# Small vector work of a two-dimensional Fourier mix moved from VectorE to GpSimd, with a new order of all operations

## The chip, the core and the metric

The kernel runs on one core of a Trainium2 chip. A core has five engines with a queue each, and every queue is worked through in order: TensorE (PE, with its weight loads shown apart as PEld), VectorE (DVE), ScalarE (ACT), GpSimd (POOL) and SyncE (SP). SP here only issues transfers. Matmuls write to PSUM, eight banks of 128 x 512 floats; DVE and ACT copy results from there to SBUF, and POOL is given only operands in SBUF.

The metric is device time in microseconds of one execution. Three runs of the kernel before gave 113.83, 114.42 and 114.73 us, median 114.42.

## The reference

```
def _A_ref(x, w_r, w_i):                      # _B_ref is the same
    X = rfft2(x.astype(float32), axes=(-2, -1))
    X = X * (w_r + 1j * w_i)
    return irfft2(X, s=(S, D), axes=(-2, -1)).astype(bfloat16)

x = A_x                                       # 1 x 2048 x 1024, bfloat16
g = sigmoid((x * gate_w).sum(-1, keepdims=True))
return g * _A_ref(x, A_w_r, A_w_i) + (1 - g) * _B_ref(x, B_w_r, B_w_i)
```

Both branches transform the same input; `B_x` is not used. So one forward transform serves both, its result is multiplied by two sets of complex weights, and the inverse transform of both is mixed by a gate per row.

## The kernel before, in words

The 2048 rows are split as 128 x 16 and the 1024 columns by symmetry into quarters, so that every transform becomes a chain of matmuls with constant matrices. Even and odd columns of the spectrum are apart from the first step on (`e` and `o`; later `par` 0 and 1).

*Folds.* For each of 16 slices `s1` and each half, `F1:s:par:bank` (L336) multiplies the input with a cosine and sine matrix. The result in PSUM has two parts whose sum and difference are wanted (`fold`, L422, two operations of 256 columns). For most, ACT or DVE copies one part to a scratch tile `wx` (`FC`, L201 on ACT, L203 on DVE) and DVE folds the other from PSUM with it (`FD`); for eight of them both parts are copied (`FX`) and POOL folds (`FP`).

*Products.* Sixteen units `n` follow, eight even and eight odd. Per unit: `F2` (L528) twice, evictions `T`; `F3` (L569), eviction `X`; on DVE the product `P:n` (`prod`, L586, 128 x 4096), which multiplies `X` with the weights of both branches. Column 0 of the product is special: a small matmul `Y` (L599, L601) and a small DVE product `NA` (`patch_mul`, L609) make its two terms in a buffer `np` of which there are two in turn, and the patch sum `N` (`patch`, L615, 16 columns) adds them into the product tile. Then `J:n` (L632) runs the first step of the inverse transform from the patched product. Its result is evicted in two halves `R`, and stored to a scratch tensor in DRAM (`H`, L654). The product tile has three buffers.

`F3` needs a negated copy `wn` of a constant; `neg:engine:from:to` (L280) makes it in two parts, 256 and 768 columns.

*The gate.* `gc` (L285 to L297) prepares coefficients from `gate_w` on POOL; `GH`, `GC`, `Gt`, `GK`, `GZ` bring the row sums to all partitions, `GS` (L485, ACT) takes the sigmoid into `EA`. Then, for four groups of four slices, `GA:engine:first` (L515) multiplies `EA` with a constant matrix and `GB` (L519) subtracts it from that matrix into `EB`, 128 x 512 each: eight operations.

*The end.* `L:par:v` (L665) loads the scratch back with rows and columns exchanged, once every `H` of that half has landed. `V` (L675) applies `EA` and `EB`, which mixes the branches; eviction `VC`; the last step is `C` or `U` (L712, L703). Even results are evicted to `EV` (`E`, `ES`, `EF`, or `EX` with sums `EQ`, L806). Odd results are added to and subtracted from them: `OR` (L826) on DVE straight from PSUM; `QD` (L833, DVE) with `QP` (L838, DVE or POOL); or `OC` with `OP` (L822, POOL). `S:v` (L847) stores two slices.

What sets the order is one string, `ORDER`, of such tokens. The program is recorded token by token, each engine's queue keeps that order, and semaphores follow the data. A token carries the engine (`A`, `D`, `P`, or `S` for a transfer) and the PSUM bank where there is a choice. The operations that the change moves:

```
Q[e].tensor_scalar(t, s, -1.0, None, ALU.mult)                         # neg
Q[e].tensor_tensor(Ps[n]...[:, :, 0], t[:, :, 0], t[:, :, 1], ALU.add) # N
Q[e].tensor_tensor(C["EA"][:, s], C["EA"][:, s], E4, ALU.mult)         # GA
Q[e].tensor_tensor(C["EB"][:, s], E4, C["EA"][:, s], ALU.subtract)     # GB
```

Here `E4` is the constant `E` repeated four times. All operands lie in SBUF.

Of the kernel before, what the change touches and what calls it, by code (L numbers as in the profile page):

```python
# [29 lines left out]
FC:11:e:A FD:9:o W:S:1 c:S:WJ:0:4 c:S:EZ FC:10:e:A F1:13:e:5 FD:9:e FD:11:e c:S:WJ:4:16 FX:7:o:A F1:12:e:1 FP:5:o FD:10:e  # L30
F1:8:o:4 F1:15:e:7 FC:13:e:A FC:12:e:A FD:13:e F1:14:e:3 F1:14:o:2 F1:6:o:5 W:S:0 W:S:7 FC:8:o:A FC:15:e:A FP:7:o F1:12:o:6
FD:12:e F1:13:o:0 FD:15:e F1:15:o:1 W:S:2 FC:14:e:A FX:6:o:A FC:14:o:A FD:14:e FD:8:o neg:D:0:4 F2:1:0:3 FC:12:o:A FC:13:o:A
F1:10:o:7 F2:0:1:5 FC:15:o:A T:1:0:A F2:1:1:4 FC:10:o:A FD:13:o FD:12:o F2:0:0:0 F1:11:o:3 T:0:1:A neg:D:4:16 FD:15:o T:1:1:A
T:0:0:A c:S:FD:1:2 F3:1:4 F3:0:0 F2:2:0:6 FC:11:o:A pw:P FD:10:o FD:14:o X:1:A F2:4:0:7 FD:11:o F2:3:0:2 W:S:3 P:1:b W:S:10
FP:6:o X:0:A F2:2:1:5 T:2:0:A F2:3:1:4 F2:4:1:3 T:2:1:A T:3:0:A Y:0:1 Y:1:0 F3:2:5 NA:1:D P:0:b GH:2 T:3:1:A X:2:A T:4:1:A
F3:3:3 N:1:D NA:0:D T:4:0:A J:1:6:0 GC:A Gt:5 X:3:A P:2:b GK:D N:0:D R:1:1:A Y:2:4 Y:3:2 R:1:0:A F2:7:0:3 NA:2:D NA:3:D
F2:5:0:5 F2:5:1:1 T:5:0:A P:3:b T:5:1:A F3:4:6 F2:7:1:2 X:4:A T:7:0:A J:0:0:4 T:7:1:D N:3:D R:0:1:A N:2:D R:0:0:D J:3:2:6
R:3:0:A R:3:1:D P:4:b GZ:0:0 F3:5:4 GS:0 X:5:A Y:4:7 NA:4:D F2:6:1:6 J:2:0:2 T:6:1:A R:2:1:A GZ:1:4 R:2:0:D Y:5:6 N:4:D GS:1
# [5 lines left out]
T:12:0:A F3:11:6 T:12:1:A J:8:4:2 P:10:b T:14:1:A X:11:A F2:13:0:1 F2:14:0:0 F3:12:6 T:14:0:D R:8:0:A R:8:1:A X:12:A H:5:0
H:5:1 H:7:1 H:7:0 H:6:0 H:6:1 T:13:0:D W:S:12 F2:13:1:0 L:0:0 L:0:7 L:0:1 J:9:2:4 T:13:1:A L:0:4 L:0:2 R:9:0:A P:11:b
J:10:0:6 L:0:5 R:10:0:A R:9:1:D F2:15:1:3 V:0:0:1:2 F3:14:0 R:10:1:A X:14:A T:15:1:A J:11:4:6 V:0:0:0:0 F2:15:0:3 L:0:6 H:8:1
R:11:1:A H:8:0 R:11:0:A P:12:b VC:0:0:1:D T:15:0:A C:0:0:1:2 VC:0:0:0:D P:14:b F3:13:6 E:0:1:D J:12:0:4 V:0:2:1:3 X:13:A
R:12:1:A H:9:0 V:0:1:1:7 C:0:0:0:6 V:0:2:0:4 VC:0:1:1:A C:0:1:1:7 VC:0:2:1:A F3:15:2 VC:0:2:0:A R:12:0:D P:13:b EX:1:1:A
J:14:0:4 H:10:1 H:9:1 X:15:A R:14:1:A H:10:0 H:11:0 H:12:1 E:0:0:D J:13:6:2 P:15:b R:14:0:A V:0:1:0:5 R:13:0:A H:12:0 H:11:1
R:13:1:D C:0:2:1:4 J:15:0:6 VC:0:1:0:A EX:2:1:A R:15:0:A GB:D:8 R:15:1:D C:0:1:0:5 EX:1:0:A V:0:6:0:4 C:0:2:0:3 EQ:2:1:0:D  # L50
V:0:6:1:1 VC:0:6:0:A V:0:5:1:0 H:14:1 V:0:5:0:5 EX:2:0:D H:14:0 H:13:1 H:13:0 C:0:6:0:7 VC:0:6:1:A VC:0:5:1:A H:15:0 E:6:0:A
H:15:1 VC:0:5:0:A C:0:6:1:4 C:0:5:1:1 E:6:1:A L:0:3 EQ:2:0:0:D ES:5:1:D L:1:3 EQ:1:1:1:P EQ:1:1:0:P V:0:4:1:6 V:0:4:0:2
V:0:7:1:5 C:0:5:0:3 EQ:2:1:1:P EQ:1:0:1:P VC:0:4:1:A EF:5:1 VC:0:4:0:D ES:5:0:D L:1:1 L:1:0 C:0:4:1:0 EQ:2:0:1:P EF:5:0
C:0:4:0:7 V:0:7:0:6 VC:0:7:1:A C:0:7:1:4 V:0:3:1:5 VC:0:7:0:D V:0:3:0:1 C:0:7:0:3 ES:4:1:A ES:4:0:A EF:4:0 EX:7:1:D
VC:0:3:1:A C:0:3:1:7 VC:0:3:0:A EX:7:0:A V:1:3:1:5 V:1:3:0:2 C:0:3:0:3 E:3:1:D L:1:5 L:1:6 L:1:7 L:1:2 VC:1:3:1:A VC:1:3:0:A
EQ:1:0:0:P EQ:7:1:0:P C:1:3:1:7 EQ:7:0:1:P C:1:3:0:2 EF:4:1 E:3:0:A EQ:7:0:0:P QD:3:1:1 V:1:1:1:0 L:1:4 QD:3:0:1 VC:1:1:1:A
V:1:1:0:1 V:1:0:0:6 U:1:1:1:0 VC:1:1:0:A VC:1:0:0:A V:1:0:1:3 C:1:0:0:6 QD:3:1:0 QD:3:0:0 U:1:1:0:5 VC:1:0:1:A V:1:6:1:2
OC:1:0:A EQ:7:1:1:P QP:3:1:1:D C:1:0:1:3 VC:1:6:1:A OR:1:1:1 OR:1:1:0 V:1:5:0:1 V:1:6:0:5 V:1:5:1:2 QD:0:0:1 QD:0:0:0
# [853 lines left out]
```

## Time and profile before

| | |
|---|---|
| median of three runs | 114.42 us |
| the profiled execution | 113.75 us, span 111.9 us |
| PE busy | 97.9 us (87%) |
| DVE busy | 99.3 us (89%) |
| ACT busy | 86.0 us (77%) |
| POOL busy | 40.7 us (36%) |
| DVE product L586, 16 times | 36.4 us, 2.28 us each |
| DVE patch sum L615, 8 times | 1.5 us, 0.22 us each |
| DVE gate operations L515 and L519, 8 times | 3.3 us, 0.42 us each |
| DVE negation L280, twice | 0.83 and 0.34 us |

The span is the part of an execution from its first to its last instruction in the profile; 1.85 us of the execution's time lie around it. An operation's duration is longer than what it takes of its engine, because the next one starts before the former has ended; the distance between two starts is what it costs the engine. Busy shares are means over stages with different limits, so the stages have to be read apart. In a row of the timeline the columns are start, duration, engine, line, operation, output and inputs by the program's names with partitions x elements and type, and the count; a bracket gives idle time before and what ended it. In a row of the groups the busy time of the group, the mean duration in nanoseconds and the idle time before follow the count.

### The profile page before, as it was taken

How to read it: one execution, taken by the hardware profiler on the slowest of the kernel's cores; microseconds unless marked ns; L12 is line 12 of the kernel's file. 1: busy time of each engine (PE TensorE's matmuls, PEld its weight loads, DVE VectorE, ACT ScalarE, POOL GpSimd, SP SyncE). 2: the span in 40 equal slices, each digit the busy share in tenths (PEclk: the TensorE clock that was granted, in tenths of full speed). 3: DMA queues.
4: the chain of work that ended last, by engine and by line, in shares of the span. 5: the costliest groups of instructions: out<-in, count | busy, mean ns of one | idle time of the engine just before them, and what ended most of it. 6: DMA issues, size and time to landing. Idle time of an engine off the chain costs nothing.

```text
span 111.9 us, 3817 instructions
## 1 busy us (share of the span) xinstructions
PE 97.9 (87%) x1559; PEld 69.9 (62%) x1559; DVE 99.3 (89%) x159; ACT 86.0 (77%) x141; POOL 40.7 (36%) x63
## 2 busy tenths in 40 slices
...
DVE  0079899999999999999999999999959799999970
ACT  4174597999999999999999999999975965554400
POOL 1079999500000000000000000054740689999970
...
DMA packets 17794, 36.79 MB, mean 329 GB/s; under 512 B 1904, under 2 KB 10736, under 8 KB 17776
## 3 DMA queue, kind: packets, MB, share of 16 engines
...
q8 instruction: 12, 0.20, 0.7%
...
q14 instruction: 6, 0.05, 0.1%
...
## 4 chain that ended last, share of the span: by engine, by line
DVE 31%; PE 30%; DMA 16%; issue 8%; POOL 6%; ACT 4%; SPq 1%; DVEq 1%; ACTq 0%; POOLq 0%
DVE p L586 13%; PE ps L675 10%; DMA sc<-rl 9%; DVE y L422 9%; PE ps L712 7%; DMA re<-sc 6%; PE ps L703 5%; POOL y L422 5%; PE ps L245 3%; DVE ot L826 3%; ACT rl L201 2%; PE ps L632 2%; DVE rl L203 1%; SPq L665 1%; ACT X L201 1%
## 5 line engine op out<-in xcount | busy, mean ns | idle before, releaser
L806 POOL TENSOR_TENSOR re<-wx 128x256 f32<-128x256 f32 x10 | 8.8, 900 | 60.6 <-ACT wx L201 53.5
L201 ACT CAST rl<-ps 128x1024 bf16<-128x1024 f32 x24 | 23.9, 1043 | 1.2 <-PE ps L632 0.7
L201 ACT CAST V<-ps 128x512 bf16<-128x512 f32 x28 | 15.6, 602 | 7.6 <-PE ps L675 4.9
L201 ACT COPY wx<-ps 128x256 f32<-128x256 f32 (+1 forms) x38 | 15.3, 458 | 7.9 <-PE ps L336 4.2
L632 PE MATMUL ps<-p,wj 32*64 32x512 bf16 x512 | 17.7, 380 | 2.9 <-DVE re L203 1.0
L528 PE MATMUL ps<-fd,y 128*128 128x256 bf16 x128 | 17.3, 273 | 1.7 <-DVE T L203 0.6
L586 DVE TENSOR_TENSOR p<-X,ro 128x4096 bf16<-128x4096 bf16 x8 | 18.2, 2280 | 0.0
L422 DVE TENSOR_TENSOR y<-ps,wx 128x256 bf16<-128x256 f32 x48 | 16.6, 415 | 1.5 <-ACT wx L201 1.5
L201 ACT CAST X<-ps 128x1024 bf16<-128x1024 f32 x16 | 16.8, 1057 | 0.5 <-DVE p L586 0.2
L336 PE MATMUL ps<-f,re 128*128 128x128 bf16 x256 | 15.3, 220 | 1.1 <-ACT wx L201 1.1
L336 PEld LDWEIGHTS <-re 128*128 128x128 bf16 x256 | 14.8, 99 | 2.0 <-issue 1.7
L201 ACT CAST T<-ps 128x512 bf16<-128x512 f32 x27 | 15.6, 623 | 0.3 <-PE ps L528 0.2
L528 PEld LDWEIGHTS <-y 128*128 128x128 bf16 x128 | 11.4, 97 | 6.5 <-issue 4.7
L632 PEld LDWEIGHTS <-wj 32*64 32x64 bf16 x512 | 8.4, 103 | 9.1 <-issue 5.9
L422 POOL TENSOR_TENSOR y<-wx 128x256 bf16<-128x256 f32 x16 | 11.1, 731 | 5.4 <-DVE wx L203 5.4
L838 POOL TENSOR_TENSOR ot<-pq 128x512 bf16<-128x512 f32 x9 | 12.0, 1361 | 0.5 <-DVE pq L833 0.5
L712 PE MATMUL ps<-ig,V 128*128 128x256 bf16 x88 | 12.2, 273 | 0.0
L569 PE MATMUL ps<-T,wf 64*64 64x512 bf16 (+1 forms) x128 | 10.0, 333 | 1.5 <-ACT rl L201 0.9
L826 DVE TENSOR_TENSOR ot<-re,ps 128x512 bf16<-128x512 f32 x16 | 9.9, 675 | 0.0
L703 PE MATMUL ps<-ig,V 128*128 128x512 bf16 x40 | 9.9, 379 | 0.0
L203 DVE CAST rl<-ps 128x1024 bf16<-128x1024 f32 x8 | 9.7, 1218 | 0.1
L586 DVE TENSOR_TENSOR p<-X,wx 128x4096 bf16<-128x4096 bf16 x4 | 9.1, 2283 | 0.0
...
## 6 DMA issues: line engine op xcount, KB each, us to landing
...
```

The source lines that it names most:

```text
L201: nc.scalar.copy(out=out, in_=in_)
L203: Q[e].tensor_copy(out=out, in_=in_)
L336: nc.tensor.matmul(o, lhsT=lh, rhs=rh, start=(h == 0), stop=(h == 1))
L422: Q[e].tensor_tensor(yo[:, v, k:k + n, s1, :], a.rearrange("p (k c) -> p k c", c=4), b.rearrange("p (k c) -> p k c", c=4), op)
L528: nc.tensor.matmul(ps[:, v * 256:v * 256 + 256], lhsT=y[:, v, par, b, 2 * t:2 * t + 2, :, :].rearrange("p j s c -> p (j s c)"), rhs=C["FD" ...
L586: nc.vector.tensor_tensor(p[:], xb, wb, ALU.mult)
L632: nc.tensor.matmul(o, lhsT=lh, rhs=src[r, ri, wi, tt], start=(q == 0), stop=(q == 3))
L675: nc.tensor.matmul(ps[:, ch * 128:ch * 128 + 128], lhsT=RR[par][:, v, ch // 2, s, c0 + 256 * ab:c0 + 256 * ab + 128], rhs=Ew[:, s1, :], st ...
L703: nc.tensor.matmul(ps, lhsT=Vs[par, v][:, s, ch, :], rhs=rh, start=(ch == 0), stop=(ch == 3))
L712: nc.tensor.matmul(ps[:, o:o + 256], lhsT=Vs[par, v][:, s, ch, :], rhs=g[:, o:o + 256], start=(ch % 2 == 0), stop=(ch % 2 == 1))
L826: nc.vector.tensor_tensor(otile(v)[:, s, h, :], EV[:, v, s], PS["O", 1, v, s], (ALU.add, ALU.subtract)[h])
L838: Q[e].tensor_tensor(otile(v)[:, :, h, 256 * g:256 * g + 256], t[:, :, 0], t[:, :, 1], (ALU.add, ALU.subtract)[g])
```

## The change

Only `ORDER` differs; all functions stay. The counts by engine:

| | before | after |
|---|---|---|
| `neg` | 2 DVE | 2 POOL |
| `N`, patch sums | 8 DVE | 1 DVE, 7 POOL |
| `GA` | 4 DVE | 2 DVE, 2 POOL |
| `GB` | 4 DVE | 1 DVE, 3 POOL |
| `FC` | 1 DVE, 23 ACT | 3 DVE, 21 ACT |
| `T` | 5 DVE, 27 ACT | 8 DVE, 24 ACT |
| `R` | 8 DVE, 24 ACT | 7 DVE, 25 ACT |
| `E` | 3 DVE, 3 ACT | 1 DVE, 5 ACT |
| `EX` | 2 DVE, 4 ACT | 1 DVE, 5 ACT |
| `EQ` | 2 DVE, 10 POOL | 4 DVE, 8 POOL |
| `QP` | 3 DVE, 9 POOL | 2 DVE, 10 POOL |

All other operations keep their number and engine (`VC` is 4 on DVE and 28 on ACT in both, but before `P:15` two were on DVE and now one is). Banks are dealt anew. The gate's coefficients `gc` come ahead of POOL's first fold and ahead of the small memset of `tab`, which ACT's first activation reads. Most weight loads `W` come earlier in SP's queue. In DVE's queue the stretch from `P:1` to `P:15` was

```
P:1 NA:1 P:0 N:1 NA:0 P:2 GK N:0 NA:2 NA:3 P:3 T:7:1 N:3 N:2 R:0:0 R:3:1 P:4 NA:4 R:2:0 N:4 NA:5 P:5
GA:12 GA:0 N:5 P:7 T:9:1 GA:4 NA:7 P:6 NA:6 N:7 N:6 T:10:1 P:8 GB:12 R:6:0 GA:8 GB:4 P:9 GB:0 P:10
T:14:0 T:13:0 P:11 R:9:1 P:12 VC:0:0:1 VC:0:0:0 P:14 E:0:1 R:12:0 P:13 E:0:0 P:15
```

and is now

```
P:1 NA:1 P:0 NA:0 P:2 NA:2 NA:3 GK P:3 T:7:1 R:0:0 R:3:1 P:4 NA:4 R:2:0 P:5 NA:5 N:5
P:7 NA:7 P:6 NA:6 GA:0 GA:12 T:9:1 T:10:1 GB:0 P:8 R:6:0 P:9 T:12:0 P:10
T:13:0 T:13:1 P:11 R:9:1 P:12 T:15:1 VC:0:0:0 T:15:0 P:14 R:12:0 P:13 P:15
```

while POOL, which had nothing between `FP:6` and the first `EQ`, now has

```
N:1 N:0 N:3 N:2 N:4 N:7 GB:12 N:6 GA:8 GB:8 GA:4 GB:4
```

The last 14 operations of POOL are ten `QP` and four `OP`; before there were nine and four. The core of the diff:

```
-warm:8 c:A:F1 x:S:0:1 x:S:1:1 F1:0:o:0 F1:0:e:5 F1:1:e:3 F1:1:o:1 c:A:gws FX:0:o:D x:S:2:2 tab:A x:S:4:2 F1:2:e:2 x:S:6:2
...
-NA:7:D P:6:b H:4:0 H:4:1 NA:6:D F3:9:4 N:7:D N:6:D T:10:1:D J:7:6:0 P:8:b X:9:A R:7:1:A J:6:2:4 R:7:0:A GB:D:12 R:6:0:D
-F3:10:0 R:6:1:A F2:11:0:7 GA:D:8 X:10:A T:11:0:A F2:12:0:2 F2:11:1:5 F2:12:1:0 F2:14:1:1 GB:D:4 P:9:b GB:D:0 T:11:1:A
...
+warm:8 c:A:F1 x:S:0:1 x:S:1:1 c:A:gws gc:P F1:0:e:7 F1:0:o:5 x:S:2:2 tab:A x:S:4:2 F1:1:o:6 x:S:6:2 FC:0:e:D FD:0:e x:S:8:2
...
+neg:P:0:4 F1:10:e:3 FX:7:o:A FP:4:o F1:10:o:4 FP:7:o F1:14:e:5 FC:13:e:A FC:10:e:A F1:12:e:7 F1:15:e:0 FD:13:e F1:6:o:6
+F1:13:o:1 FC:14:e:A neg:P:4:16 FC:15:e:A pw:P FD:10:e FC:10:o:A FD:14:e FC:12:e:A FD:15:e F1:12:o:2 FD:12:e FD:10:o F1:14:o:3
...
+GA:D:12 T:9:1:D T:10:1:D F3:9:4 GB:D:0 H:4:0 X:9:A H:2:0 P:8:b J:7:6:0 R:7:0:A GB:P:12 N:6:P GA:P:8 J:6:2:4 GB:P:8 R:7:1:A
+F2:11:0:7 GA:P:4 R:6:1:A F2:11:1:6 R:6:0:D H:5:1 F2:12:1:0 H:4:1 H:5:0 H:7:0 H:7:1 T:11:1:A F3:10:2 T:11:0:A P:9:b F2:12:0:4
...
+P:14:b J:12:0:4 VC:0:1:1:A X:13:A V:0:2:1:3 C:0:0:0:6 C:0:1:1:7 R:12:1:A V:0:2:0:5 VC:0:2:1:A F3:15:2 EX:1:1:A VC:0:2:0:A
...
+OR:7:1:1 OR:4:1:1 OR:4:1:0 S:S:6 S:S:7:1 S:S:4
```

More of the change, by code (lines that the diff above doesn't have):

```diff
@@ L30 @@
[L30 to L38, printed above, removed]
@@ L44 @@
[L44 to L53, printed above, removed]
@@ L54 @@
[L54 to L58, printed above, removed]
@@ L64 @@
-OP:4:0:0 OR:7:1:0 S:S:7:1 OR:4:1:0 OR:4:1:1 S:S:4
+warm:8 c:A:F1 x:S:0:1 x:S:1:1 c:A:gws gc:P F1:0:e:7 F1:0:o:5 x:S:2:2 tab:A x:S:4:2 F1:1:o:6 x:S:6:2 FC:0:e:D FD:0:e x:S:8:2
+F1:1:e:3 FX:0:o:D FC:1:e:D c:S:WF:0:4 c:S:E FX:1:o:A x:S:10:2 F1:3:e:6 x:S:12:2 x:S:14:2 F1:2:o:5 c:S:WF:4:16 FC:3:e:A FD:1:e
+F1:2:e:2 FD:3:e F1:3:o:4 F1:5:e:7 F1:4:e:1 c:S:FD:0:1 FX:2:o:A F1:5:o:3 F1:7:e:5 c:S:w0 c:S:WJ:0:4 FP:1:o F1:6:e:6 c:S:EZ
+c:S:PM W:S:0 FC:2:e:A FP:0:o FD:2:e W:S:1 c:S:FD:1:2 W:S:7 W:S:3 W:S:2 W:S:5 W:S:4 c:S:WJ:4:16 FC:5:e:A FD:5:e FC:4:e:A
@@ new lines @@
+F1:9:o:2 F1:8:o:0 FC:7:e:A FD:4:e FC:6:e:A FX:5:o:A F1:8:e:7 FC:9:o:A FP:2:o FP:5:o FD:7:e FD:6:e FC:8:o:A FX:3:o:A F1:9:e:3
+F1:4:o:1 F1:7:o:5 FC:9:e:A FD:9:o FC:8:e:A FD:8:o FD:9:e FD:8:e F1:11:e:2 FX:4:o:A FC:11:e:A FD:11:e F1:13:e:6 FP:3:o
+neg:P:0:4 F1:10:e:3 FX:7:o:A FP:4:o F1:10:o:4 FP:7:o F1:14:e:5 FC:13:e:A FC:10:e:A F1:12:e:7 F1:15:e:0 FD:13:e F1:6:o:6
+F1:13:o:1 FC:14:e:A neg:P:4:16 FC:15:e:A pw:P FD:10:e FC:10:o:A FD:14:e FC:12:e:A FD:15:e F1:12:o:2 FD:12:e FD:10:o F1:14:o:3
+FX:6:o:A FC:12:o:A FD:12:o F1:15:o:0 F2:1:0:7 FC:15:o:D FC:14:o:A FC:13:o:A FD:14:o FD:13:o F2:0:0:5 F2:1:1:4 F2:0:1:6
@@ new lines @@
+F1:11:o:2 T:1:0:A T:0:0:A T:1:1:A T:0:1:A FC:11:o:A F3:1:4 F3:0:6 X:1:A FD:15:o X:0:A FD:11:o P:1:b F2:2:0:1 F2:3:1:3 Y:1:0
+F2:2:1:5 F2:3:0:2 T:2:0:A NA:1:D Y:0:7 FP:6:o T:2:1:A T:3:1:A F2:4:1:6 F2:4:0:1 N:1:P F3:2:4 T:3:0:A T:4:0:A GH:3 X:2:A
+F3:3:4 T:4:1:A P:0:b NA:0:D GC:A J:1:6:0 F2:7:0:3 X:3:A P:2:b N:0:P R:1:1:A Y:2:4 Gt:5 Y:3:2 R:1:0:A NA:2:D F2:5:0:4 T:5:0:A
+F2:5:1:0 NA:3:D F3:4:6 GK:D P:3:b F2:7:1:2 T:7:1:D N:3:P N:2:P T:5:1:A J:0:0:4 X:4:A T:7:0:A J:3:2:6 R:0:1:A R:0:0:D W:S:6
+R:3:1:D W:S:10 W:S:8 P:4:b GZ:0:0 F3:5:4 R:3:0:A GS:0 W:S:9 c:S:IG W:S:11 Y:4:7 F2:6:1:6 X:5:A T:6:1:A J:2:0:2 F2:6:0:6
@@ new lines @@
+T:12:1:A F3:11:6 T:12:0:D F2:14:0:0 X:10:A X:11:A F2:14:1:1 J:8:4:2 T:14:1:A H:6:0 H:6:1 T:14:0:A W:S:13 L:0:0 F3:12:6
+F2:13:0:1 L:0:1 L:0:6 L:0:2 R:8:0:A R:8:1:A P:10:b GB:P:4 F2:13:1:0 J:9:2:4 X:12:A R:9:0:A T:13:0:D T:13:1:D L:0:5 J:10:0:6
+R:10:0:A L:0:7 L:0:4 F2:15:1:3 V:0:0:1:2 P:11:b H:8:0 H:8:1 R:9:1:D F3:14:0 R:10:1:A X:14:A J:11:4:6 VC:0:0:1:A P:12:b H:9:0
+H:9:1 V:0:0:0:1 H:10:0 H:10:1 R:11:1:A F2:15:0:2 T:15:1:D C:0:0:1:0 VC:0:0:0:D R:11:0:A V:0:1:1:3 E:0:1:A F3:13:6 T:15:0:D
+P:14:b J:12:0:4 VC:0:1:1:A X:13:A V:0:2:1:3 C:0:0:0:6 C:0:1:1:7 R:12:1:A V:0:2:0:5 VC:0:2:1:A F3:15:2 EX:1:1:A VC:0:2:0:A
```

30 lines of the change are left out of this document (18 added, 12 removed).

## The prediction

> **What bounds the kernel now.** I read the page's forty slices first, one digit for the busy tenths of 2.8 us:
>
> ```profile
> DVE  0079899999999999999999999999959799999970
> ACT  4174597999999999999999999999975965554400
> POOL 1079999500000000000000000054740689999970
> ...
> DVE p L586 13%; PE ps L675 10%; DMA sc<-rl 9%; DVE y L422 9%; PE ps L712 7%; DMA re<-sc 6%; PE ps L703 5%; POOL y L422 5%; PE ps L245 3%; DVE ot L826 3%; ACT rl L201 2%; PE ps L632 2%; DVE rl L203 1%; SPq L665 1%; ACT X L201 1%
> ```
>
> There are three stages. To 25 us DVE folds, beside POOL. From 25 to 77 us DVE has next to no idle time and ACT some 1.6 us, while POOL stands still: these two engines are the bound, and the product (L586) is the longest item of the chain that ended last, whose shares are the last line. From 77 us PE is full until its matmuls end near 104; behind it DVE and POOL finish the output together. That last point decides much here, so I took the ends from the timeline of each engine:
>
> ```profile
> 99.24 6.19 POOL L838 TENSOR_TENSOR ot<-pq 128x512 bf16<-128x512 f32 x5
> 105.60 2.73 POOL L822 TENSOR_TENSOR ot<-re,wx 128x512 bf16<-128x512 f32 x2 [0.17 <-ACT wx L201]
> ...
> 105.90 2.47 DVE L826 TENSOR_TENSOR ot<-re,ps 128x512 bf16<-128x512 f32 x4
> ```
>
> POOL ends at 108.33, DVE at 108.37; the last store takes the rest to 111.9. Since 90.91 POOL has run 13 operations with hardly a gap.
>
> Next the question that the change raises: can POOL work beside DVE? Before, POOL does nothing during the products but at their end, so I put both timelines side by side there, and where DVE made the negated constants beside POOL's folds:
>
> ```profile
> 72.13 2.28 DVE L586 TENSOR_TENSOR p<-X,y 128x4096 bf16<-128x4096 bf16 x1
> 74.33 0.68 DVE L203 COPY re<-ps 128x512 f32<-128x512 f32 x1
> 74.93 2.28 DVE L586 TENSOR_TENSOR p<-X,y 128x4096 bf16<-128x4096 bf16 x1
> ...
> 73.43 1.57 POOL L806 TENSOR_TENSOR re<-wx 128x256 f32<-128x256 f32 x1 [52.39 <-ACT wx L201]
> 76.77 1.03 POOL L806 TENSOR_TENSOR re<-wx 128x256 f32<-128x256 f32 x1 [1.78 <-DMA sc<-rl]
> ...
> 19.61 1.42 POOL L422 TENSOR_TENSOR y<-wx 128x256 bf16<-128x256 f32 x2
> ...
> 20.29 0.83 DVE L280 TENSOR_SCALAR wn<-wf 128x256 bf16<-128x256 bf16 x1
> ...
> 22.36 0.34 DVE L280 TENSOR_SCALAR wn<-wf 128x768 bf16<-128x768 bf16 x1
> ```
>
> POOL's L806 takes 0.72 us at its shortest. The one issued at 73.43, inside a product, ends at 75.00: the product's 74.33 plus 0.67. The next, issued inside the product that gives way at 77.13, ends at 77.80, again 0.67 later. DVE waits likewise: 256 columns of L280 took 0.83 us beside a fold that ended at 21.03, 768 columns 0.34 with POOL idle. So a POOL operation that reads SBUF and a DVE operation with both inputs in SBUF exclude each other, whole instruction by whole instruction. DVE's evictions from PSUM show no such wait.
>
> The Trainium skill (SBUF — State Buffer, Who interferes with whom) says the same: GpSimd and a DVE instruction with two SBUF inputs share a port that is locked for the whole instruction, and whichever issues first keeps it. The trace agrees in these three places; that order of issue decides speaks for the forecast below against its first rival.
>
> **The change, part by part.** Sums are made on the profiled execution (113.75 us, span 111.9). DVE durations are pitches, start to start: product 2.20 (25.28 to 27.48), T or V eviction 0.60, R eviction 1.13, gate operation 0.35, patch sum 0.09.
>
> *Folds.* The two negations leave DVE: 0.75 and 0.27, -1.0. Two more FC copies come to it at 0.38, +0.8. On POOL the negations are covered by their use: the first F3 needed them at 23.06, and the nearest rows (L320, 0.35 for 32 columns; L422, 0.73 for 256) put them at 0.35 to 2.1 us each on an engine idle from 21.03. The gate's coefficients now stand ahead of POOL's first fold and ahead of the memset that ACT's first activation waits for. Their input lands at 1.14 + 3.6 = 4.7 us; POOL's first arithmetic was seen at 6.20, so that chain of 1.1 us ends between 5.8 and about 8.5, against ACT's first copy at 6.32. Cover is ACT's idle time in this stage (3.5 us) and the copies that DVE now makes for itself first; without it, up to 1 us. I take -0.2, bounds -0.7 and +1.0.
>
> *Products, work of DVE up to the last one.* Seven patch sums, 7 x 0.09 = -0.6. Of the gate's operations, seven stood before the last product and three do now: -1.4. Evictions dealt anew: T from 5 to 8 (+1.8), V from 2 to 1 (-0.6), E from 2 to 0 (-1.25), R 6 as before: -0.05. Together -2.05. ACT's share of the same stretch falls by 3 T (1.5) and an FC (0.4) and grows by a V and an E (1.0): -0.9. X:15 ended 0.66 before the product that uses it began, so -1.5 is the most that ACT allows.
>
> *What the moved work costs in its new place.* The rows for POOL:
>
> ```profile
> L838 POOL TENSOR_TENSOR ot<-pq 128x512 bf16<-128x512 f32 x9 | 12.0, 1361 | 0.5 <-DVE pq L833 0.5
> L822 POOL TENSOR_TENSOR ot<-re,wx 128x512 bf16<-128x512 f32 x4 | 5.3, 1329 | 0.2 <-ACT wx L201 0.2
> ...
> L313 POOL TENSOR_TENSOR wp<-eb 128x32 f32<-128x32 bf16 x2 | 0.5, 264 | 0.0
> L293 POOL TENSOR_TENSOR gh<-gh 128x4 f32<-128x4 f32 x1 | 0.2, 203 | 0.1
> ```
>
> A gate operation of 512 columns is 1.27 us there (the shortest L838; 0.72 from half its width is the floor, two folds, 1.46, the ceiling), a patch 0.2 to 0.26. Each falls to POOL after a product and holds the port until done; only evictions run beside it. GB:12 has T:9:1 and T:10:1 (1.2), GA:8 has R:6:0 (1.13), GB:8 has T:12:0 (0.6), GA:4 two T (1.2), GB:4 has R:9:1 (1.13): what sticks out is 0.1 + 0.15 + 0.65 + 0.1 + 0.15 = 1.15. The patches N:3, N:2 and N:4 lie beside evictions and cost nothing. N:1, N:0, N:7 and N:6 have only an NA of 0.1 or a gate operation next to them and push DVE by some 0.2 each, 0.8. NA:3 writes the small buffer that N:0 read, so DVE now waits there for POOL, 0.3. Sum +2.2; nothing if all were hidden, 5 x 1.27 + 7 x 0.26 = 8.2 if nothing were. By the 2.6 cycles per element at 1.2 GHz of the Trainium skill (GPSIMD Engine Reference, Elementwise — side-by-side cycle accounting) a gate operation would be an estimated 1.1 us and this sum some 0.6 less; no row has that operation on POOL.
>
> What queues behind the patches is PE: each J waits for its N and every later matmul for J. For N:1, N:0 and N:7 nothing changes, since DVE also made them only after the next product (P:0 stands between NA:1 and N:1 at 27.58 to 29.78). N:6 is new: it stands on POOL behind GB:12.
>
> So the last product ends at -0.2 - 2.05 + 2.2, about as before.
>
> *The end.* From J:15 to the odd half's first block PE has 24 blocks of 0.444 instead of 25: -0.45. POOL makes 14 of the last operations instead of 13: +1.27, less one collision with DVE's L838 (about 0.35, from 4.19 for three): +0.9. DVE has one L838 less, 0.75, but its end no longer counts, POOL's does. Weight loads, stores and scratch loads keep their numbers; the last scratch store waits on R:15:1, now on ACT, which I cost at nothing: the load behind it was issued at 83.59, landed 3.5 later and was first used at 87.5, so 0.4 is what a slip beyond that would begin to cost. The banks dealt anew I put at zero, plus or minus 0.5 (PE's longest waits for an eviction are 0.6 to 1.0).
>
> Total +0.4: 114.15 for the profiled execution. That lies 0.67 below the median of the runs shown (114.42; 113.83 to 114.73), to which I carry the difference: **114.8 us**, no change. A measurement of this kernel can tell about 1% from no change: 113.28 to 115.56.
>
> **The rivals.** *The patch that waits behind POOL's gate work, slower.* Place: the end of GB:0 on DVE. N:6 has then asked for the port and P:8 is ready. If P:8 gets it, N:6 waits 2.2 us, J:6 follows, and R:6:0, next on DVE after P:8, waits for N:6 (0.25), J:6 (1.07) and two hand-overs (0.2): 1.5 us, less the 0.15 that GA:8 no longer sticks out. That is 116.15; with each product boundary after it met as badly, up to 118. For it: before never shows both engines asking at one moment. Against: N:6 asks first. It decides the sign of a measurable result: the other costs leave 0.75 us to the bound, this one takes 1.35.
>
> *The port costs little, faster.* If POOL's work falls beside evictions as DVE slips later, the 2.2 goes, ACT's limit of -1.5 holds, and 114.42 - 1.5 + 0.45 = 113.4; with an end that DVE and not POOL sets, 112.5. Middle 112.9. For it: ACT copies enough in the window; against: GB:8 has only one T beside it.
>
> *The moved operations do not matter,* because the new deal of evictions and banks outweighs them: its terms (+1.8, -0.6, -1.25) cancel by my count, and the time stays inside the forecast.
>
> **How the numbers follow.** Forecast and the third rival, 113.28 to 115.56: 0.40. The waiting patch, 115.56 to 118: 0.36; still slower, from more of the 8.2: 0.04. The cheap port, 112.4 to 113.28: 0.20. The range, 112.8 to 117.6, leaves out half of the last and the ends above. Faster by over 1%: 0.20; within: 0.40; slower: 0.40.
>
> **What would show it.** L615 on POOL with a mean far above 0.26 and L515/L519 above 1.27 (time waiting for the port); DVE's products longer than 2.28 in the mean; PE waits at L632 put down to POOL; POOL ending after DVE, by about a microsecond. The forecast is wrong if the first product does not start within 0.7 us of 25.28, if ACT's first copy is past 8.5, or if DVE idles for more than 1 us before R:6:0.

## The result and the profile after

The changed kernel takes 114.87 us in the median (113.88 to 116.09, 16 runs), the kernel before 113.97 us beside it (113.72 to 114.73, 16 runs). The ratio is 1.0058, with a 95% interval of 1.0035 to 1.0082: within 1%, with a small loss, since the interval stays above 1. The ratios here and below leave out runs over 1.5% above the fastest of the same kernel (here the one of 116.09 us), and they can stand a few tenths of a per cent from the quotient of two medians. The profiled execution took 115.02 us (before 113.75), its span is 113.2 us (before 111.9).

First the forty slices of the page after and the chain of work that ended last:

```profile
DVE  0098999999998999999999999997678897999960
POOL 3149699964911000779996000016622299999940
...
DMA re<-in_x_dram 9%; DMA ro<-sc 8%; PE ps L703 8%; DVE p L586 7%; ACT rl L201 6%; PE ps L675 5%; PE ps L632 5%; DMA sc<-rl 5%; DVE y L422 4%; ACT T L201 4%; DMA gws<-in_gw_dram 3%; DVE rl L203 3%; ACT X L201 3%; PE ps L336 3%; PE ps L528 2%
```

GpSimd (POOL) now has work in the slices 9 to 13 and 17 to 22, where before it stood still (a part of that is waiting, which the slices count as busy), and VectorE (DVE) is full from the third slice on, which was a 7. In the chain the product L586 has fallen from 13% to 7%, and two transfers have come in that were not among its shares: the input `re<-in_x_dram` with 9% and the scratch load of the odd half, `ro<-sc`, with 8%.

The groups of the page (columns: line, engine, operation, output and inputs with shapes, count; busy us and mean ns; idle time before):

```profile
L615 POOL TENSOR_TENSOR p<-np 128x16 bf16<-128x16 f32 x7 | 7.9, 1135 | 16.3 <-DVE np L609 13.5
...
L586 DVE TENSOR_TENSOR p<-X,wx 128x4096 bf16<-128x4096 bf16 x4 | 10.5, 2624 | 0.0
```

A patch sum of 16 columns takes 1135 ns in the mean on GpSimd, though the shortest takes 0.26 us: the rest is waiting for VectorE. And the four products on `wx` take 2624 ns in the mean instead of 2283: here VectorE waits for GpSimd. Where this happens, the timelines of VectorE and, behind the dots, of GpSimd show (columns: start, duration, engine, line, operation, count; in brackets idle time and what ended it):

```profile
24.50 2.29 DVE L586 TENSOR_TENSOR p<-X,ro 128x4096 bf16<-128x4096 bf16 x1
...
53.76 2.28 DVE L586 TENSOR_TENSOR p<-X,wx 128x4096 bf16<-128x4096 bf16 x1
...
56.55 2.65 DVE L586 TENSOR_TENSOR p<-X,wx 128x4096 bf16<-128x4096 bf16 x1
...
60.32 3.27 DVE L586 TENSOR_TENSOR p<-X,wx 128x4096 bf16<-128x4096 bf16 x1
...
76.38 0.68 DVE L203 CAST V<-ps 128x512 bf16<-128x512 f32 x1
...
15.56 0.85 POOL L280 TENSOR_SCALAR wn<-wf 128x256 bf16<-128x256 bf16 x1
...
19.13 2.13 POOL L280 TENSOR_SCALAR wn<-wf 128x768 bf16<-128x768 bf16 x1
...
50.05 0.44 POOL L615 TENSOR_TENSOR p<-np 128x16 bf16<-128x16 f32 x1
...
53.80 3.26 POOL L519 TENSOR_TENSOR eb<-e,ea 128x512 bf16<-128x512 bf16 x1
57.01 3.20 POOL L515 TENSOR_TENSOR ea<-ea,e 128x512 bf16<-128x512 bf16 x1
60.29 1.15 POOL L519 TENSOR_TENSOR eb<-e,ea 128x512 bf16<-128x512 bf16 x1
```

The first product starts at 24.50 (before 25.28), the last gives way at 76.38 (before 77.13). The product stage is thus 51.88 us long, and was 51.85. `GB:8`, issued at 53.80 beside a product, ends only at 57.06; the product issued at 56.55 waits for it and takes 2.65. `GB:4` is issued at 60.29, 0.03 us ahead of the product at 60.32: it runs at once, 1.15 us, and the product takes 3.27.

The rest is lost behind the products. From the last product to the end of the span it was 34.8 us before and is now 36.8. Of VectorE and, behind the dots, GpSimd in that stretch:

```profile
89.23 2.48 DVE L833 TENSOR_TENSOR pq<-re,ps 128x512 f32<-128x512 f32 x4 [0.42 <-PE ps L712]
...
96.10 1.88 DVE L833 TENSOR_TENSOR pq<-re,ps 128x512 f32<-128x512 f32 x3 [0.68 <-PE ps L712]
...
99.70 1.81 DVE L838 TENSOR_TENSOR ot<-pq 128x512 bf16<-128x512 f32 x1
101.44 7.85 DVE L826 TENSOR_TENSOR ot<-re,ps 128x512 bf16<-128x512 f32 x13
...
97.22 2.51 POOL L822 TENSOR_TENSOR ot<-re,wx 128x512 bf16<-128x512 f32 x2
99.69 6.64 POOL L838 TENSOR_TENSOR ot<-pq 128x512 bf16<-128x512 f32 x5
106.29 2.49 POOL L822 TENSOR_TENSOR ot<-re,wx 128x512 bf16<-128x512 f32 x2
```

VectorE ends at 109.29 (before 108.37), GpSimd at 108.78 (before 108.33). In between VectorE's L838, 0.7 us elsewhere, took 1.81 (99.70): GpSimd's L838 had been issued 0.01 us earlier, at 99.69. And VectorE stood 0.68 us for a matmul (96.10). TensorE's timeline has, two microseconds ahead of that, the one wait of this stretch, for a scratch load of the odd half:

```profile
94.15 0.23 PE L675 MATMUL ps<-ea,ro 128*128 128x128 bf16 x1 [0.41 <-DMA ro<-sc]
```

Before, TensorE did not wait for these loads at all. The chain of work that ended last, in order of time, now passes through this load and not through the L838 (columns: start, duration, what):

```profile
85.17 8.93 DMA ro<-sc
...
94.15 0.62 PE ps L675 x8
...
103.13 3.89 PE ps L703 x17
```

From 94.15 it stays on TensorE until 107.02 and ends with VectorE's last sums.

### The profile page after: what moved, and what is told of

The parts are those of the page before. It is cut to its first block, busy times and chain, and to the rows that moved or that the text cites. A ratio compares the mean times of both kernels' runs of the same rounds, so it can differ in the third digit from the quotient of the medians.

```text
span 113.2 us, 3831 instructions
## 1 busy us (share of the span) xinstructions
PE 98.8 (87%) x1557; PEld 70.7 (62%) x1559; DVE 98.7 (87%) x147; ACT 86.3 (76%) x140; POOL 61.8 (55%) x76
## 4 chain that ended last, share of the span: by engine, by line
PE 26%; DMA 25%; DVE 19%; ACT 15%; issue 9%; SPq 2%; DVEq 1%; ACTq 0%
DMA re<-in_x_dram 9%; DMA ro<-sc 8%; PE ps L703 8%; DVE p L586 7%; ACT rl L201 6%; PE ps L675 5%; PE ps L632 5%; DMA sc<-rl 5%; DVE y L422 4%; ACT T L201 4%; DMA gws<-in_gw_dram 3%; DVE rl L203 3%; ACT X L201 3%; PE ps L336 3%; PE ps L528 2%
## 5 line engine op out<-in xcount | busy, mean ns | idle before, releaser
L201 ACT CAST rl<-ps 128x1024 bf16<-128x1024 f32 x25 | 24.7, 1059 | 1.1 <-PE ps L632 1.1
L632 PE MATMUL ps<-p,wj 32*64 32x512 bf16 x512 | 17.6, 379 | 3.4 <-ACT rl L201 1.2
L586 DVE TENSOR_TENSOR p<-X,ro 128x4096 bf16<-128x4096 bf16 x8 | 18.3, 2286 | 0.0
L806 POOL TENSOR_TENSOR re<-wx 128x256 f32<-128x256 f32 x8 | 6.2, 787 | 20.9 <-PE ps L675 14.6
L615 POOL TENSOR_TENSOR p<-np 128x16 bf16<-128x16 f32 x7 | 7.9, 1135 | 16.3 <-DVE np L609 13.5
L336 PE MATMUL ps<-f,re 128*128 128x128 bf16 x256 | 15.9, 225 | 0.8 <-DMA re<-in_x_dram 0.6
L336 PEld LDWEIGHTS <-re 128*128 128x128 bf16 x256 | 15.5, 102 | 1.7 <-DMA re<-in_x_dram 1.0
L838 POOL TENSOR_TENSOR ot<-pq 128x512 bf16<-128x512 f32 x10 | 13.3, 1366 | 2.1 <-DVE pq L833 2.1
L632 PEld LDWEIGHTS <-wj 32*64 32x64 bf16 x512 | 8.2, 103 | 9.7 <-issue 4.9
L201 ACT CAST T<-ps 128x512 bf16<-128x512 f32 x24 | 13.8, 644 | 0.4 <-PE ps L528 0.2
L586 DVE TENSOR_TENSOR p<-X,wx 128x4096 bf16<-128x4096 bf16 x4 | 10.5, 2624 | 0.0
L203 DVE CAST rl<-ps 128x1024 bf16<-128x1024 f32 x7 | 8.5, 1219 | 1.3 <-PE ps L632 1.2
```

The source lines that it names most:

```text
L201: nc.scalar.copy(out=out, in_=in_)
L203: Q[e].tensor_copy(out=out, in_=in_)
L336: nc.tensor.matmul(o, lhsT=lh, rhs=rh, start=(h == 0), stop=(h == 1))
L586: nc.vector.tensor_tensor(p[:], xb, wb, ALU.mult)
L632: nc.tensor.matmul(o, lhsT=lh, rhs=src[r, ri, wi, tt], start=(q == 0), stop=(q == 3))
L838: Q[e].tensor_tensor(otile(v)[:, :, h, 256 * g:256 * g + 256], t[:, :, 0], t[:, :, 1], (ALU.add, ALU.subtract)[g])
```

## The experiments

The theory after this first reading was: VectorE and GpSimd shut each other out, instruction by instruction, while both read two operands from SBUF; what the moves save on VectorE they take back there, and the new order loses in the end. The rivals were that the moves are worth their whole saving and the order spends it, and that the moves do not matter. The ratios below are against the kernel before on the same chips, each with its 95% interval. Stages, starts and ends are read from one profiled execution of each kernel.

**Parts of the moves, undone in the new order.** `e1_gate_back`:

```
-GB:P:12 ... GA:P:8 ... GB:P:8 ... GA:P:4 ... GB:P:4
+GB:D:12 ... GA:D:8 ... GB:D:8 ... GA:D:4 ... GB:D:4
```

> The changed kernel with its five gate operations back on DVE, at the same places of the order; all else as changed. Theory A (the port, sized from the trace after): DVE gains back 5 x 0.35 = 1.75 of work and loses the waits for POOL that the trace shows on P:10 (0.37), P:11 (0.99) and GB:0 (0.05), so 1.4: +0.3, ratio to before about 1.009, P:10 and P:11 at 2.28. Theory B (the gate work on POOL is what makes the change slower): at or below before, ratio 1.000 or less. Theory C (the new order and banks make it slower, not the moves): ratio stays within 0.003 of 1.006.

Measured: 114.50 us, 1.0069 (1.0043 to 1.0094), which rules out theory B and leaves A and C. P:10 and P:11 are back at 2.28. In the profiled execution (115.84 us, the slowest of its twelve) the product stage took 52.26 us, against 51.88.

`e2_patch_back`; four of the patches need another place, to suit VectorE's queue:

```
-N:1:P N:0:P N:3:P N:2:P N:4:P N:7:P N:6:P
+N:1:D (behind P:0)  N:0:D (behind P:2)  N:4:D (ahead of P:5)  N:6:D (behind GA:12)  N:3:D N:2:D N:7:D
```

> The changed kernel with its seven patch sums back on DVE, N:1, N:0, N:4 and N:6 set behind P:0, P:2, R:2:0 and GA:12 on DVE. Theory A: DVE gains 7 x 0.09 = 0.6 and loses the 0.15 that NA:3 waited: +0.4, ratio about 1.010. Theory B (patches on POOL hold PE, since each J waits for one): faster than the change, ratio 1.001 or less, and fewer waits of L632 for anything but evictions. Theory C: within 0.003 of 1.006.

Measured: 114.92 us, 1.0089 (1.0059 to 1.0119), the stage 52.86 us. The timeline of VectorE in e2 shows the same five gate operations on GpSimd, hit worse than after, since they are now met by three products in a row:

```profile
50.41 3.24 DVE L586 TENSOR_TENSOR p<-X,wx 128x4096 bf16<-128x4096 bf16 x1
...
54.71 3.21 DVE L586 TENSOR_TENSOR p<-X,wx 128x4096 bf16<-128x4096 bf16 x1
...
58.45 2.64 DVE L586 TENSOR_TENSOR p<-X,wx 128x4096 bf16<-128x4096 bf16 x1
```

Over the 2.28 of an undisturbed product that is 0.96 + 0.93 + 0.36 = 2.25 us of waiting, where after has 0.37 + 0.99 = 1.36. Undoing a part brings no time back; neither ratio can be told from that of after, and theory B falls here too.

**The moves alone, in the old order.** `e3_gate_alone` and `e4_patch_alone`:

```
e3  -GB:D:12  GA:D:8  GB:D:8  GA:D:4  GB:D:4      +GB:P:12  GA:P:8  GB:P:8  GA:P:4  GB:P:4
e4  -N:1:D  N:0:D  N:3:D  N:2:D  N:4:D  N:7:D  N:6:D    +N:1:P  N:0:P  N:3:P  N:2:P  N:4:P  N:7:P  N:6:P
```

> The kernel before with only the same five gate operations on POOL, tokens where they were. Theory A: DVE saves 5 x 0.35 = 1.75; on POOL each waits for the end of a product and then keeps DVE from the next one for what no eviction covers: by the old order 0 for GA:4, 0.5 for GB:12, 0.4 for GA:8, 0.15 for GB:4, 0.9 for GB:8: 2.0. Sum +0.2, ratio 1.000 to 1.004, products after an uncovered operation up to 1.1 longer than 2.28. Theory B: ratio 1.006 or more. If there were no such wait, 0.985 to 0.990.

> The kernel before with only the same seven patch sums on POOL. Theory A: DVE saves 0.6, NA:3 and one or two products wait 0.1 to 0.3 each: -0.3, ratio 0.995 to 1.000; L615 on POOL has a mean of 1 us and more, since those that fall inside a product wait for its end. Theory B (PE is held): ratio 1.004 or more.

Measured: e3 115.38 us, 1.0147 (1.0110 to 1.0184); e4 113.92 us, 1.0002 (0.9976 to 1.0029). In e3 the product stage is 53.44 us, 1.59 more than before, although four of the five operations (4 x 0.35 = 1.4 us) have left it: they cost 3.0 us. The timelines of VectorE and GpSimd in e3 say where (lines are one lower in this kernel):

```profile
44.16 1.18 DVE L614 TENSOR_TENSOR p<-np 128x16 bf16<-128x16 f32 x1
45.22 2.28 DVE L585 TENSOR_TENSOR p<-X,ro 128x4096 bf16<-128x4096 bf16 x1
...
48.12 2.54 DVE L585 TENSOR_TENSOR p<-X,ro 128x4096 bf16<-128x4096 bf16 x1
...
50.68 1.16 DVE L614 TENSOR_TENSOR p<-np 128x16 bf16<-128x16 f32 x2
...
52.30 2.64 DVE L585 TENSOR_TENSOR p<-X,wx 128x4096 bf16<-128x4096 bf16 x1
...
43.99 1.27 POOL L518 TENSOR_TENSOR eb<-e,ea 128x512 bf16<-128x512 bf16 x1 [3.02 <-DVE ea L514]
45.23 3.28 POOL L514 TENSOR_TENSOR ea<-ea,e 128x512 bf16<-128x512 bf16 x1
48.47 4.33 POOL L518 TENSOR_TENSOR eb<-e,ea 128x512 bf16<-128x512 bf16 x2
```

Patch sums that take 0.22 (one) and 0.34 (two) alone take 1.18 and 1.16 here, products 2.54 and 2.64: 0.96 + 0.82 + 0.26 + 0.36 = 2.4 us in four places. In two more, VectorE stands for TensorE ahead of an eviction, 0.21 and 0.29 us. Theory A had the waits at 2.0 us in all, so its ratio of at most 1.004 was too low: in the old order the five operations on GpSimd do make the kernel slower. The patches on GpSimd gain next to nothing: e4's stage is 51.55, 0.3 shorter, where seven patch sums are worth 0.6. No product of e4 is longer for them, but two evictions wait 0.23 and 0.19 us for TensorE.

**All moves apart from the order.** `e5_order_alone` is the changed kernel with all 14 moves back on VectorE (the diffs of e1 and e2 together, and `neg:D`); `e6_moves_alone` is the kernel before with all 14 on GpSimd (e3 and e4 together, and `neg:P`).

> The changed kernel with all fourteen operations (two negations, seven patch sums, five gate operations) back on DVE: only the new order, the new deal of evictions and the new banks remain. Theory C (these make it slower, the moves gain a little): ratio to before 1.008 to 1.014, and P:15 ends later than in the changed kernel. Theory B (the moves cost): 1.003 or less.

> The kernel before with all fourteen operations on GpSimd, tokens where they were. If the costs of the parts add (patches 1.000, gate operations 1.015, negations -1.0 us on DVE at the first product, so about -0.004): 1.008 to 1.014. If the moves were free of the port: 0.975 to 0.985.

Measured: e5 115.37 us, 1.0107 (1.0065 to 1.0150); e6 115.51 us, 1.0120 (1.0058 to 1.0182). So the order with its banks and evictions costs 1.1%, the moves 1.2% on the old order; both together cost 0.6%, not 2.3%. On the new order the moves are worth about 1.0058 / 1.0107 = 0.995 (the two intervals overlap, so even the sign of this half per cent is loose; a loss of 1.2%, as on the old order, would have put after at 1.023, far above its interval). The same instructions on the same engine lose in one order and gain, or lose nothing, in another.

e5 and e6 also bear on the start. In e5, with the negations on VectorE, the first product starts at 25.38; in e6, with them on GpSimd and the old order, at 24.5. One execution says little here, but all runs shown here agree: with the negations on VectorE in the old order (before, e3, e4, e9, e10, e12) the first product starts between 24.84 and 25.55, with them on GpSimd in either order (after, e1, e2, e6, e7, e8, e11) between 23.99 and 24.89. The means differ by 0.8 us. So the negations bring the start forward, and the new order does not.

**Two suspected losses at the end.** `J:15` starts 0.7 us behind the last product. TensorE's timeline after puts it to VectorE's eviction of the bank that it writes:

```profile
77.11 1.07 PE L632 MATMUL ps<-p,wj 32*64 32x512 bf16 x32 [0.29 <-DVE V L203]
```

`e7_bank` gives that eviction to ScalarE, ahead of another one:

```
-V:0:1:0:0 R:13:0:A EQ:1:1:0:P C:0:2:1:4 P:15:b VC:0:1:0:D
+V:0:1:0:0 VC:0:1:0:A R:13:0:A EQ:1:1:0:P C:0:2:1:4 P:15:b
```

> The changed kernel with one eviction, VC:0:1:0, made by ACT ahead of R:13:0 instead of by DVE behind P:15. It frees the bank that J:15 writes. In the changed kernel J:15 starts at 77.11 although P:15 ends at 76.38. If that bank is what J:15 waits for: J:15 starts within 0.2 of the end of P:15, some 0.6 earlier, and the time falls by 0.3 to 0.6, ratio 1.001 to 1.003. If not (the wait is the semaphore after P:15 or something else): no change, 1.006.

TensorE's timeline in e7:

```profile
76.41 0.41 PE L632 MATMUL ps<-p,wj 32*64 32x512 bf16 x4
77.19 1.06 PE L632 MATMUL ps<-p,wj 32*64 32x512 bf16 x28 [0.37 <-ACT rl L201]
```

Measured: 115.47 us, 1.0098 (1.0061 to 1.0136), no gain. Four matmuls of `J:15` start at 76.41, the other 28 at 77.19, now behind ScalarE's eviction of the other banks that `J:15` writes. The wait moved from one eviction to the next, and in that execution TensorE also waited 0.67 us for a scratch load of the odd half, at 87.86.

`e8_tail` takes away the L838 that met GpSimd's at 99.70, and gives VectorE two sums straight from PSUM for it:

```
-QP:0:1:1:D  OC:1:0:A  OP:1:0:0  OP:1:0:1
+QP:0:1:1:P  OR:1:0:0  OR:1:0:1        (behind QD:6:0:1)
```

> The changed kernel with QP:0:1:1 on POOL instead of DVE and, in exchange, OR:1:0:0 and OR:1:0:1 on DVE (one input in PSUM) instead of OC:1:0 on ACT with OP:1:0:0 and OP:1:0:1 on POOL; the two OR fill the 0.7 that DVE waits for PE at 96.1. If DVE's end is set by the 1.1 that its L838 waits for POOL's port at 99.7: DVE ends some 1.0 earlier and POOL one operation (1.27) earlier, ratio 0.995 to 0.998. If the end is set by PE: no change, 1.006.

Measured: 114.42 us, 1.0029 (0.9991 to 1.0067); the profiled stretch from the first `QD` to the end of VectorE is 19.3 us instead of 20.06. VectorE now waits for nothing but TensorE:

```profile
104.17 2.48 DVE L826 TENSOR_TENSOR ot<-re,ps 128x512 bf16<-128x512 f32 x4 [0.24 <-PE ps L703]
106.80 2.48 DVE L826 TENSOR_TENSOR ot<-re,ps 128x512 bf16<-128x512 f32 x4 [0.15 <-PE ps L703]
```

The loss is half that of after by the estimate, though the two intervals overlap, and VectorE's end, 109.28, is that of after (109.29). That the meeting at 99.70 cost VectorE 1.1 us is read from the trace; that taking it out is worth 0.3% is not shown, and three other runs speak against so much. e1, e2 and e5 have the same order behind the last product as after. In them TensorE waits for no load of the odd half, VectorE does not stand 0.68 us, and the same L838 loses some 0.45 us instead of 1.1. VectorE and, behind the dots, GpSimd in e5:

```profile
100.45 1.16 DVE L838 TENSOR_TENSOR ot<-pq 128x512 bf16<-128x512 f32 x1
101.53 7.88 DVE L826 TENSOR_TENSOR ot<-re,ps 128x512 bf16<-128x512 f32 x13
...
101.01 6.66 POOL L838 TENSOR_TENSOR ot<-pq 128x512 bf16<-128x512 f32 x5
107.62 2.50 POOL L822 TENSOR_TENSOR ot<-re,wx 128x512 bf16<-128x512 f32 x2
```

| us | before | after | e1 | e2 | e5 | e8 |
|---|---|---|---|---|---|---|
| last product to first `QD` | 12.41 | 12.85 | 13.86 | 12.95 | 12.86 | 12.86 |
| first `QD` to VectorE's end | 18.83 | 20.06 | 18.85 | 18.84 | 18.85 | 19.32 |
| first `QD` to GpSimd's end | 18.79 | 19.55 | 19.54 | 19.53 | 19.56 | 19.17 |

Behind the first `QD` the new order thus costs some 0.7 us, on GpSimd, which ends last in e1, e2 and e5 (19.5; the 19.32 of e8 is 0.2 less); the 1.2 us more of VectorE stand in the profiled execution of after alone. In e5 the loss to before, 1.7 us of span, is 0.1 at the start, 0.5 in the products, 0.45 up to the first `QD` and 0.7 behind it.

**The port by itself.** All this rests on one reading, that two SBUF reads exclude each other. `e9_port_read` and `e10_port_write` were to measure it with added work on GpSimd that nothing waits for:

> The kernel before, and on GpSimd twelve additions more, each 128x512 bf16 from two SBUF constants into a scratch tile that nothing reads, in one row behind the fourth product (P:3); nothing waits for them. In e3_gate_alone five such additions cost VectorE about 3.0 us, 0.6 each. Theory (VectorE and GpSimd shut each other out while both read two SBUF operands, and each addition gets its turn between two VectorE instructions): 12 x 0.6 = 7.2 us, with bounds of 4 and 14 (12 x 1.15, none hidden): about 121 us, from 118 to 128, ratio near 1.06; VectorE shows idle gaps or long products of about 1.1 us while the additions run. Rival (what cost e3 its time were the waits for the five sums, not the reads): nobody waits here, so 114.0 +- 0.6.

> As e9, but the twelve instructions are memsets of 128x1024 bf16: GpSimd writes SBUF and reads nothing. Theory (the reads exclude each other): 114.0 +- 0.6, ratio within 1.005, products unchanged at 2.28 us. Rival (any use of SBUF by GpSimd shuts VectorE out): 12 memsets at the price of the additions, 118 to 128 us as in e9.

Their traces have no such instruction on GpSimd. The added token never came into `ORDER`, so they are the kernel before with one memset of a constant more, and say nothing on the port. What they do say is how two kernels without a difference compare: 0.9994 (0.9956 to 1.0031) and 0.9984 (0.9955 to 1.0012).

`e12_port_both` holds the work, reads and writes in one kernel:

```
+def port_probe(n, kind):
+    nc.gpsimd.tensor_copy(out=junk[0:1, 0:1], in_=p_n[0:1, 0:1])        # start after product n
+    for _ in range(6):
+        if kind == "r": nc.gpsimd.tensor_tensor(pb, pa[:, 0], pa[:, 1], ALU.add)    # 128 x 512, two SBUF operands
+        else:           nc.gpsimd.memset(pa, 0.0)                                    # 128 x 1024, writes only
-... P:3:b ...           ... P:10:b ...
+... P:3:b pp:3:r ...    ... P:10:b pp:10:w ...
```

> The traces of e9_port_read and e10_port_write have no addition and no memset of the probe on GpSimd between 21 and 73 us: the kernels as run did not hold them, and both runs are the kernel before with one memset of a constant more ahead of the products. This run holds them, in one kernel: on GpSimd six additions of 128x512 bf16 from two SBUF constants behind the fourth product (P:3), and six memsets of 128x1024 bf16 behind the product P:10, all into scratch tiles that nothing reads; nothing waits for either. Theory (the engines shut each other out where both read two SBUF operands): the additions show 2 to 4 us each instead of 1.15, VectorE loses up to 1.15 to each, by e3's 0.6 each about 3.6 us in all (1 to 7), nearly all of it between P:3 and P:10; beside the memsets the products stay at 2.28 and no gap of VectorE appears; 117.6 us, 115 to 121. Rival A (the waits for the sums cost e3 its time): 114.0 +- 0.6, products at 2.28 all along. Rival B (any use of SBUF by GpSimd shuts VectorE out): the stretch from P:10 on is longer by over 1 us too.

Measured: 116.75 us (4 runs) against 113.99, 1.026 (1.0198 to 1.0321), 2.76 us more. GpSimd's two runs of six, and, behind the dots, VectorE beside the first and beside the second:

```profile
34.83 11.51 POOL L854 TENSOR_TENSOR pb<-pa 128x512 bf16<-128x512 bf16 x6
...
62.65 5.98 POOL L856 MEMSET pa<- 128x1024 bf16 x6
...
35.14 1.01 DVE L615 TENSOR_TENSOR p<-np 128x16 bf16<-128x16 f32 x2
36.01 2.56 DVE L202 CAST rl<-ps 128x1024 bf16<-128x1024 f32 x2
...
40.78 1.22 DVE L202 CAST rl<-ps 128x1024 bf16<-128x1024 f32 x1
41.91 1.17 DVE L615 TENSOR_TENSOR p<-np 128x16 bf16<-128x16 f32 x1
...
45.26 1.71 DVE L515 TENSOR_TENSOR ea<-ea,e 128x512 bf16<-128x512 bf16 x2
...
63.58 2.29 DVE L586 TENSOR_TENSOR p<-X,wx 128x4096 bf16<-128x4096 bf16 x1
...
66.92 2.29 DVE L586 TENSOR_TENSOR p<-X,y 128x4096 bf16<-128x4096 bf16 x1
```

The rows of before that answer to the three that are too long are 0.30 (two patch sums), 0.22 (one) and 0.76 (two gate operations); here they take 1.01, 1.17 and 1.71. That is 0.71 + 0.95 + 0.95 = 2.6 us, and the stretch from the end of P:3 to the start of P:10 is 25.65 us instead of 23.10, 2.55 more. So three of six additions were paid for, and three ran free, beside the evictions at 36.01 and 40.78, which read PSUM. L609, which takes one operand from PSUM, kept its 0.18 us throughout. Beside the six memsets (5.98 us) the products stay at 2.29 and the evictions at 1.22; from the start of P:10 to the end of the last product it is 19.11 us, against 19.15 before. Both rivals fall: nobody waits for these additions and they cost 0.4 to 0.5 us each in the mean, and writes cost nothing. The Trainium skill (SBUF — State Buffer, Who interferes with whom) has it so: a VectorE instruction with two SBUF inputs contends with a GpSimd instruction that reads SBUF, not with one that only writes it. The trace agrees, with 2.6 us for the one and none for the other.

**What is left when the costly part is taken out.** `e11_neg_patch` is the kernel before with the negations and the patches on GpSimd and the five sums on VectorE:

```
-neg:D:0:4  neg:D:4:16  N:1:D  N:0:D  N:3:D  N:2:D  N:4:D  N:7:D  N:6:D
+neg:P:0:4  neg:P:4:16  N:1:P  N:0:P  N:3:P  N:2:P  N:4:P  N:7:P  N:6:P
```

> The kernel before with the two negations and the seven patch subtractions on GpSimd, in their old places; the five sums stay on VectorE, and order, banks and evictions are the old ones. Theory (the negations bring the first product 0.7 us forward, as in e6_moves_alone, the patches cost VectorE nothing, and the sums are what cost): first product at 24.5 to 24.7, last one done at 76.2 to 76.5 instead of 77.13, 113.2 us, ratio 0.993, below both kernels. Rival (the gain ahead of the products is given back in the end, where VectorE and GpSimd are both full): 114.0, ratio 0.998 to 1.002.

Measured: 113.44 us against 113.99, 0.9948 (0.9917 to 0.9979), below both kernels. VectorE's timeline: the first product starts at 23.99, earlier than was expected, and the last one gives way 1.0 us earlier than before.

```profile
76.14 1.22 DVE L202 CAST rl<-ps 128x1024 bf16<-128x1024 f32 x1
...
89.92 2.48 DVE L832 TENSOR_TENSOR pq<-re,ps 128x512 f32<-128x512 f32 x4 [1.79 <-PE ps L711]
```

But in the execution that was profiled (114.1 us, slower than this kernel's median) VectorE then stood 1.79 us for TensorE ahead of 89.92, which was 89.54 before. TensorE's timeline has the cause, a wait for the scratch load of the odd half:

```profile
87.93 0.23 PE L674 MATMUL ps<-ea,ro 128*128 128x128 bf16 x1 [1.19 <-DMA ro<-sc]
```

The first of these loads was issued at 83.3, where before it was 83.6: it came 0.3 us forward, not 1.0, and took at least 4.6 us to land instead of 3.5. With 4 MB to load at some 410 GB/s, the rate of the window's slices, the eight loads take about 10 us. So the gain ahead of the products is there, and the scratch load is what is late next; which part of the gain it takes in the median run, one profile cannot tell.

## Why the prediction was right

The forecast of 114.8 us and of no change was met: 114.87, 1.0058. Its sum of +0.4 us was +1.3 in the profiled execution and +0.9 between the medians, and two of its steps were off, by 0.6 and 1.6 us, in opposite directions. That they nearly cancel is luck. So in part is the nearness of 114.8 to 114.87: the median of three runs on which the forecast stood, 114.42, was 0.45 above the median of sixteen, 113.97, and the difference came out 0.5 larger than forecast.

- *The port.* That GpSimd and VectorE exclude each other was right (e3, e12). But one of the three places does not show the rule as it was put: L280 reads one operand from SBUF, not two. Its 0.83 us beside a fold shows that it waited too; "both inputs in SBUF" rested on the two rows of L806 alone.
- *Folds, "I take -0.2".* Too small: -0.78 in the profiled executions, just past the bound of -0.7. The term that failed is "two more FC copies come to it at 0.38, +0.8". They stand at the very start, where VectorE had waited 1.5 us for ScalarE's copies; that wait is now 0.2, so the copies cost nothing. The negations' saving, "-1.0", came for the most part: 0.8 between the means of the runs with and without it. Their price on GpSimd, "0.35 to 2.1 us each", measured 0.85 and 2.13, and was covered. The step on ScalarE held: its first copy came at 7.00, not past 8.5.
- *Products, "-2.05" and "+2.2".* Right in the sum, 51.88 against 51.85. Of the price the gate's part was about 1.4 instead of 1.15: `GB:8` pushed a product by 0.37 (I had 0.65), and `GB:4` by 0.99 where I had 0.15, because I put it beside `R:9:1` behind P:11, while it was issued 0.03 us ahead of P:11. The patches cost less than "0.8" and "0.3": the one delay next to them is 0.16, where `NA:2` and `NA:3` start at 31.45 behind a product that gave way at 31.29, and it lies ahead of `NA:2`, which does not use the buffer of N:0. In their place came a wait of 0.37 for TensorE ahead of the eviction at 35.04. That a gate operation takes 1.27 was a little high; free of waiting it took 1.15, closer to the estimated 1.1 worked out from the Trainium skill (GPSIMD Engine Reference, Elementwise — side-by-side cycle accounting).
- *"The last product ends about as before."* 0.75 earlier, from the folds.
- *The end, "PE -0.45", "POOL +0.9", "DVE's end no longer counts, POOL's does".* This is the step that failed: the stretch behind the last product grew by 2.0 us, not by 0.45. "PE -0.45" did not come: from the end of `J:15` to the first `QD` it was 11.05 us instead of 11.21, and `J:15` itself starts 0.73 us behind the product (0.14 before), held by an eviction. From the last product to that `QD` it is thus 12.85, and was 12.41; "banks dealt anew, zero, plus or minus 0.5" missed that 0.6. "POOL +0.9" was nearly right: from the first `QD` to GpSimd's end it is 0.76 more, and as much in e1, e2 and e5. That GpSimd's end counts held in those three, but not in the profiled execution of the change: there VectorE stood 0.68 us for TensorE, then lost 1.1 us where its remaining L838 met GpSimd's, and ended 0.5 behind GpSimd. The last 0.4 us of the 2.0 lie behind VectorE's end, up to the end of the span.
- *"The last scratch store", nothing, with a cover of 0.4.* It was less covered than that: TensorE waited 0.41 us at 94.15, two microseconds ahead of VectorE's wait of 0.68. In e1, e2 and e5 neither wait is there, nor the late meeting of the two L838. That the load caused them is read from this comparison, not tried. The prediction went by the first load alone, and this is a later one.
- *The rivals.* The waiting patch did not occur: `N:6` was issued at 50.05, took 0.44, and P:8 came at 50.41; order of issue decided, as argued. The cheap port did not occur either. The third came nearest in a way not meant: the order alone costs 1.1% (e5), and the moves earn about half of it back by the estimates, whose intervals overlap.
- *What was to show it.* L615 at 1135 ns and L515/L519 at 3252 and 1854 ns on GpSimd, the products on `wx` at 2624: as said. No wait at L632 is put down to GpSimd. GpSimd ending after VectorE: not in the profiled execution, but in e1, e2 and e5, by 0.7 us. The condition of the first product, within 0.7 us of 25.28, was missed by 0.08, less than executions of one kind differ; the forecast held all the same, for the end took back what the start gave.
